# Attention followed by two mixture layers: another spread of the query rows over the partitions, other steps for score pairs and loads, another order of the first loads

## The chip, the cores and the metric

The kernel runs on one NeuronCore of one Trainium2 chip. The metric is the time of one execution on the device in microseconds (us), lower is better. The profile is one execution on the same chip type, whose own time stands beside its span below.

## The reference

Two batches, 12 heads, 448 positions, head size 64. Scores are mixed over the heads before the softmax (`w_pre`) and the probabilities are mixed over the heads after it (`w_post`); then come two dense layers of width 2048, one with ELU, one with SiLU.

```
scores = scale * q @ k.T                          # (b, h, i, j)
scores = einsum('bhij,hg->bgij', scores, w_pre)   # mix heads
attn   = exp(scores - max_j); attn = attn / (sum_j + 1e-9)
attn   = einsum('bhij,hg->bgij', attn, w_post)    # mix heads again
x      = (attn @ v) as (b*s, h*d)                 # 896 x 768
x      = elu(x @ moe_w_in) @ moe_w_out
out    = silu(x @ moe2_w_in) @ moe2_w_out
```

## The kernel before, in words

The order of every engine's work is the order of the program text (`manual_schedule`), so each engine and each queue is first in, first out.

**Query tiles and score pairs.** The 896 query rows (batch 0, then batch 1) are cut into seven tiles T = 0 to 6 of 128 rows; tile 3 holds the last 64 rows of batch 0 in partitions 0 to 63 and the first 64 of batch 1 in 64 to 127. `qk_pair(T, p)` (L128) computes the scores of heads 2p and 2p+1 for all rows of a tile into two PSUM banks, and `qk_evac` (L140) copies them, one on ScalarE and one on VectorE, into the tile `s` with one query row per partition and 12 x 448 values in it.

**Blocks and moves.** The head mixing wants (query, head) on the partitions. Each batch is therefore cut into 45 blocks of ten query rows (the last has eight), numbered through both batches, 90 in all. `move` (L153) copies one block by a DMA on SyncE's queue from `s` (ten partitions, 12 heads each) to `blk` (120 partitions, 448 values each). Where the rows of a block lie is fixed by `spread` (L40): the whole blocks of a tile lie interleaved, row i of the k-th block at partition i*n + k, where n is the number of whole blocks (12 in a full tile, 5 and 6 in the halves of tile 3), so the ten rows of one block are 12 (5, 6) partitions apart. The rows of blocks that are cut by a tile's edge, and the last eight rows of a batch, lie side by side behind them, and each such piece is a move of its own.

**Steps.** Step s of 45 handles blocks 2s and 2s+1: `premix` (L174, two PSUM banks, waits for the two moves of its blocks), row maximum (`rmax`, VectorE), exponentials (`exps`, ScalarE), `recip`, scaling of the post weights on GpSimd, and in the next step `postmix` (L212) and `post_evac`. `relayout(s + 2)` (L157) is called in step s, so moves run two steps ahead; `blk` has three buffers (`NBUF`), so a move waits until `premix` of three steps earlier has read its buffer. Step s also runs what dictionaries put there: `QK_AT` a score pair of a later tile, `X_AT` two attention-times-value pairs (`av_pair`, from step 8, mostly in even steps), `D_AT` loads on SyncE's queue: query tiles (`load_q`), the keys of batch 1 (`load_k(1, p)`), quarters of the values (`load_v`).

**Before the first step.** A tile of zeros is set, ScalarE writes one element of it (which loads its table), three matmuls of zeros run on TensorE (L290), keys of batch 0 and the first three query tiles are loaded on the SyncE and ScalarE queues, all six pairs of tile 0 are computed, the moves of steps 0 and 1 are issued, then three pairs of tile 1 (`LEAD`).

**After step 44** the two dense layers run, 36 to 96 matmuls in a row on TensorE, with weights that are loaded by SyncE.

```
for s in range(AHEAD): relayout(s)          # L296
...
premix(s); X_AT; QK_AT; postmix(s - 1); rmax(s); exps(s)
... qk_evac, recip, post_evac(s - 1); relayout(s + AHEAD); D_AT; M_AT   # L330
```

Of the kernel before, what the change touches and what calls it, by code (L numbers as in the profile page):

```python
# [7 lines left out]
F32 = mybir.dt.float32  # L8
# [4 lines left out]
AF = mybir.ActivationFunctionType  # L13
# [4 lines left out]
P = 128  # L18
B, H, S, D = 2, 12, 448, 64
# [3 lines left out]
NP = H // 2  # L23
CP = S // 4
BI = 10
# [3 lines left out]
HS = 64  # L29
BW = 5 * H  # L30
NBUF = 3
NWARM = 3
NE = 3
LEAD = 3
KO = (0, 2, 4, 1, 3, 5)
# [1 line left out]
KB = -(-S // BI)  # L37


def spread():  # L40

    tiles, blocks = [], {}
    for segs in ([(0, 0, 128)], [(0, 128, 256)], [(0, 256, 384)], [(0, 384, 448), (1, 0, 64)], [(1, 64, 192)], [(1, 192, 320)], [(1, 320, 448)]):
        T, base, of = len(tiles), 0, [None] * P
        for b, q0, q1 in segs:
            k0, k1 = -(-q0 // BI), q1 // BI
            n = k1 - k0
            for k in range(k0, k1):
                blocks[b, k] = [(T, base + k - k0, n, BI, 0)]
                for i in range(BI):  # L50
                    of[base + i * n + k - k0] = (b, k * BI + i)
            r = base + BI * n
            for x0, x1 in ((q0, k0 * BI), (k1 * BI, q1)):
                if x1 > x0:
                    blocks.setdefault((b, x0 // BI), []).append((T, r, 1, x1 - x0, x0 % BI))
                    for x in range(x0, x1):
                        of[r] = (b, x)
                        r += 1
            base += q1 - q0
        tiles.append((of, [b for b, _, _ in segs]))  # L60
    return tiles, blocks


QTILES, BLOCKS = spread()


@with_exitstack
def attn_moe_moe(ctx: ExitStack, tc: tile.TileContext, q, k, v, w_pre, w_post, w1i, w1o, w2i, w2o, out):
    nc = tc.nc
# [3 lines left out]
    def pool(name, **kw):  # L73
        cm = tc.tile_pool(name=name, reuse_waits="tile", **kw)
        return cm, cm.__enter__()

    cm_c, cp = pool("const", bufs=1, side="left")
# [3 lines left out]
    cm_w, wp = pool("qt", bufs=1, side="right")  # L81
# [5 lines left out]
    cm_ps, ps = pool("psA", bufs=1, space=PSUM)  # L87

    kpre = cp.tile([P, HS], F32, name="kpre")
    kps = cp.tile([P, H, 5], F32, name="kps")  # L90
    cp.tile([P, 24], F32, name="align2")
    vall = [ap_.tile([P, H, 4, D], F32, name=f"v{b}") for b in range(B)]
    blkb = ap_.tile([P, NBUF, 2, S], F32, name="blk")

    tiles = [(b, t) for b in range(B) for t in range(4)]
# [5 lines left out]
    qT, kT = {}, {}  # L101

    def load_q(T, eng=None, parts=(slice(0, NP),)):
        qT[T] = wp.tile([P, NP, 2 * P], F32, name=f"qt{T}", tag="qT", bufs=3).rearrange("p a b -> p (a b)")[:, :NP * P].rearrange("p (a b) -> p a b", a=NP)
        for p in parts:
            (eng or nc.sync).dma_start(qT[T][:, p], q[T, :, p])

    def load_k(b, p, eng=None):
        if b == 0:
            kT[p] = kp.tile([P, 2, S], F32, name=f"kt{p}", tag=f"kT{p}")  # L110
        (eng or nc.sync).dma_start(kT[p][:, b], k[b, p])

    def load_v(b, u, g):

        h = slice(3 * g, 3 * g + 3)
        o = slice(0, P) if u is None else slice(HS * u, HS * u + HS)
        nc.sync.dma_start(vall[b][o, h].rearrange("p h r d -> p (h r d)"), v[b, o, 768 * g:768 * g + 768])
# [10 lines left out]
    def qk_pair(T, p, where=("qk0", "qk1")):  # L128

        bs = QTILES[T][1]  # L130
        if T not in smap:
            smap[T] = (sp1, sp0)[T % 2].tile([P, H, S], F32, name=f"s{T}", tag="s")
        pq = [ps.tile([P, S], F32, name=f"pq{T}_{p}_{e}", tag=w, bufs=1) for e, w in enumerate(where)]
        for c in range(2):
            for e in range(2):
                half = slice(e * D, (e + 1) * D)
                nc.tensor.matmul(pq[e][HS * c:HS * c + HS], qT[T][half, p, HS * c:HS * c + HS], kT[p][half, bs[c % len(bs)]], start=True, stop=True, tile_position=(e * D, HS * c))  # L137
        sev.append((T, p, pq))

    def qk_evac(e):  # L140
        for T, p, pq in sev:
            o = smap[T][:, 2 * p + e]
            if e == 0:
                nc.scalar.activation(o, pq[0], AF.Copy, scale=0.125)  # L144
            else:
                nc.vector.tensor_scalar(o, pq[1], 0.125, None, op0=ALU.mult)
        if e == 1:
            sev.clear()

    seq = [(b, n) for b in range(B) for n in range(KB)]  # L150
    NB = len(seq) // 2

    def move(s, c, piece):  # L153
        T, r, d, m, i = piece
        nc.sync.dma_start(blkb[4 + H * i:4 + H * (i + m), s % NBUF, c], smap[T][r:r + d * (m - 1) + 1:d])

    def relayout(s):  # L157

        if s >= NB:
            return  # L160
        for c in range(2):
            x = BLOCKS[seq[2 * s + c]]
            for piece in x[len(x) - 1 if c == 0 else 0:]:
                move(s, c, piece)
        if s + 1 < NB:
            for piece in BLOCKS[seq[2 * s + 2]][:-1]:
                move(s + 1, 0, piece)

    def prow(s):
# [2 lines left out]
    pre, nmx, pexp, sums, kr, pst = {}, {}, {}, {}, {}, {}  # L172
# [9 lines left out]
    def rmax(s):  # L182
        n = prow(s)
        nmx[s] = ap_.tile([P, 2], F32, name=f"nmx{s}", tag="nmx", bufs=3)
        for r in range(2):
            nc.vector.tensor_reduce(nmx[s][:n, r:r + 1], pre[s][r][:n], axis=AX.X, op=ALU.max, negate=True)  # L186
# [83 lines left out]

    wz = sp0.tile([P, S], F32, name="wz", tag="s")
    nc.vector.memset(wz, 0.0)
    nc.scalar.activation(wz[0:1, 0:1], wz[0:1, 0:1], AF.Copy)
    load_k(0, 0, nc.scalar)
    load_q(0, parts=(slice(0, 2), slice(2, NP)))
    for p in range(1, NP):
        load_k(0, p, (nc.scalar, nc.sync)[p % 2])
    nc.scalar.dma_start(kpre, w_pre)
    nc.scalar.dma_start(kps.rearrange("p h i -> p (h i)"), w_post)
    load_q(1)  # L280
    load_q(2)
    for g in range(2):
        load_v(0, None, g)
    nc.gpsimd.memset(blkb[0:4], 0.0)
    for c in range(2):
        for r in range(2):
            nc.vector.memset(pbank[c][HS * (1 - r):HS * (2 - r), (4 * r + 3) * BW:(4 * r + 4) * BW], 0.0)
    for n in range(NWARM):
        pw = ps.tile([P, 4 * CP], F32, name=f"warm{n}", tag=f"pre{n % 3}", bufs=1)
        nc.tensor.matmul(pw, wz[:, :P], wz, start=True, stop=True)  # L290
    BANKS = (("qk0", "qk1"), ("pre0", "pre1"), ("pre2", "av"))
    for p in range(NP):
        qk_pair(0, p, BANKS[p % 3])
# [2 lines left out]
    for s in range(AHEAD):  # L296
        relayout(s)
# [6 lines left out]
    QK_AT, X_AT, D_AT = {}, {}, {}  # L304

    def at(d, step, f):
        d.setdefault(int(step), []).append(f)

    for T, n0 in enumerate((1 - LEAD, 4, 11, 17, 24, 30), 1):
        for p in range(LEAD if T == 1 else 0, NP):  # L310
            at(QK_AT, n0 + p, lambda T=T, p=p: qk_pair(T, p))
    for T in range(3, NQ):
        at(D_AT, (3, 9, 13, 19)[T - 3], lambda T=T: load_q(T))
    for T in range(NT_ - 1):
        for p in range(NP):
            nav = 8 + 6 * T + p // 2 * 2 if T < 5 else (38, 39, 40, 42, 43, 44)[3 * T + p // 2 - 15]
            at(X_AT, nav, lambda T=T, p=p: av_pair(T, p))
    for p in range(NP):
        at(D_AT, 6 + p, lambda p=p: load_k(1, p))
    for g in range(4):  # L320
        for u in range(2):
            for b in range(B):
                if b == 1 or g > 1:
                    at(D_AT, 2 * g + u + (16 if b else 0), lambda b=b, u=u, g=g: load_v(b, u, g))

    def run(d, s):
        for f in d.get(s, []):
            f()

    def step(s):  # L330
        if s < NB:
            premix(s)
        run(X_AT, s)
        run(QK_AT, s)
        run(F_AT, s)
        if 0 <= s - 1 < NB:
            postmix(s - 1)
        if s < NB:
            rmax(s)
            exps(s)  # L340
        two = s in X_AT
        if two:
            run(B_AT, s)
            if s < NB:
                recip(s)
            av_evac()
            av_split()
        qk_evac(0)
        qk_evac(1)
        if not two:  # L350
            run(B_AT, s)
            if s < NB:
                recip(s)
        if 0 <= s - 1 < NB:
            post_evac(s - 1)
        relayout(s + AHEAD)
        run(D_AT, s)
        run(M_AT, s)
# [230 lines left out]
    for i in range(2 * NE):  # L589
        n, j = divmod(i, 2)  # L590
# [40 lines left out]
    x1 = mo["x1"]  # L631
# [23 lines left out]
    h = {}  # L655
# [262 lines left out]
    n = NE  # L918
# [56 lines left out]
    x = [t[:, i] for t in rr for i in range(3)] + [xq[1, 5]] + [xq[1, p] for p in range(5)]  # L975
    xt[1] = {}
    for t, n_ in zip(x, "B11_0 B11_1 B11_2 T1_0 T1_1 T1_2 B21_0 B21_1 B22_0 T2_0 T2_1 B22_1 T3_0 T3_1 T4_0 T4_1 B21_2 T2_2 T3_2 T4_2 B22_2".split()):
        a, i = n_.split("_")
        xt[1][a, int(i)] = t
    for n in range(O1 + 8, I2):  # L980
        po = out_iter(n)
        if n == O1 + 9:
            y = mo["eg"][:1, 3, :1]
            nc.scalar.activation(y, y, AF.Silu)
        if po:
            c = chunks[n][2]
# [11 lines left out]
    x = [t[:, i] for t in rt for i in range(3)] + rk[:3]  # L998
# [3 lines left out]
    x = [ge[u][:, i] for u in range(2) for i in range(3)] + [gs[:, i] for i in range(6)]  # L1002
# [87 lines left out]
```

## Time and profile before

| | |
|---|---|
| median of 3 runs | 627.4 us (626.49 to 627.94) |
| the profiled execution | 626.38 us, span 624.6 us |
| TensorE matmul busy | 604.4 us (97%) |
| VectorE busy | 423.4 us (68%) |
| ScalarE busy | 363.2 us (58%) |
| GpSimd busy | 63.1 us (10%) |
| chain that ended last | PE 86%, DMA 7%, ACT 4%, DVE 2%, issue 1% |
| DMA | 82.03 MB, mean 131 GB/s |

Busy time is the union of an engine's instructions. The chain that ended last is followed back from the last instruction; its share of an engine is the time in which the program's end hung on that engine. The 45 steps take from 15 us to about 178 us of the span.

### The profile page before, as it was taken

What the parts mean: (1) busy time and instruction counts of PE and PEld (TensorE: products, weight loads), DVE (VectorE), ACT (ScalarE), POOL (GpSimd) and SP (SyncE); (2) the same over time, 40 slices, a digit from 0 to 9 for tenths busy, and PEclk for the clock granted to TensorE, in tenths of its full rate; (3) what the DMA queues carried; (4) which work ended last, traced back from release to release, by engine and by line L of the source; (5) the groups of instructions that cost most, each with busy time, mean ns of one, the idle gap of its engine ahead of it and who ended that gap; (6) DMA issues with size and microseconds to landing.
All of it is one profiled execution on the core that took longest, in us unless ns stands there. A gap on an engine that the chain in (4) does not pass through costs nothing.

```text
span 624.6 us, 14978 instructions
## 1 busy us (share of the span) xinstructions
PE 604.4 (97%) x6168; PEld 513.9 (82%) x6168; DVE 423.4 (68%) x717; ACT 363.2 (58%) x675; POOL 63.1 (10%) x117
## 2 busy tenths in 40 slices
PE   7899998998999999999999999999999999999997
PEld 3455654666689989999999999999999999999997
DVE  4766765787747799896776675599888877434420
ACT  4666765677856876657883554277676665332210
POOL 1222222226570000000000000000000000000000
PEclk9999999999999999999999999999999999999999
DMA  7586465555432235323244233434433423545300
GB/s 250 187 210 207 136 162 157 201 147 182 137 104 72 82 106 180 120 93 119 86 127 136 82 117 102 152 102 152 119 134 102 135 92 124 162 138 164 114 30 29
DMA packets 37588, 82.03 MB, mean 131 GB/s; under 512 B 4112, under 2 KB 18192, under 8 KB 37520
## 3 DMA queue, kind: packets, MB, share of 16 engines
q1 hardware_dynamic: 36656, 80.21, 41.3%
q8 instruction: 48, 0.79, 0.5%
q10 hardware_dynamic: 864, 0.87, 0.4%
q14 instruction: 20, 0.16, 0.1%
HBM read 59.05 MB, written 2.75 MB: 99 GB/s over the span
## 4 chain that ended last, share of the span: by engine, by line
PE 86%; DMA 7%; ACT 4%; DVE 2%; issue 1%; ACTq 0%; POOL 0%; DVEq 0%; SPq 0%; POOLq 0%
PE po L521 37%; PE b L795 27%; DMA blk<-s 7%; PE av L247 5%; PE pre L180 4%; PE post L219 4%; PE pq L137 3%; PE ph L507 3%; ACT pe L194 2%; PE post L507 1%; DVE nmx L186 1%; PE warm L290 1%; DVE a L123 1%; ACT gs L658 0%; ACT we L727 0%
## 5 line engine op out<-in xcount | busy, mean ns | idle before, releaser
L795 PE MATMUL b<-x,we 128*128 128x448 f32 x360 | 93.7, 363 | 0.0
L194 ACT ACTIVATE pe<-pre,nmx 124x448 f32<-124x448 f32 x90 | 56.3, 630 | 48.1 <-DVE nmx L186 47.2
L521 PE MATMUL po<-x,we 128*128 128x448 f32 x288 | 81.0, 362 | 0.0
L747 ACT ACTIVATE wr<-wr 128x768 f32<-128x768 f32 (+1 forms) x61 | 52.6, 864 | 41.9 <-DMA wr<-in_w2o_dram 26.9
L795 PEld LDWEIGHTS b<-x,we 128*128 128x128 f32 x360 | 67.5, 188 | 4.6 <-DVE we L527 0.2
L795 PE MATMUL b<-rr,we 128*128 128x448 f32 x288 | 69.5, 362 | 0.0
L478 DVE TENSOR_TENSOR we<-wc,we 128x640 fp32r<-128x640 f32 (+1 forms) x37 | 32.4, 875 | 48.3 <-ACT we L469 48.2
L219 PEld LDWEIGHTS post<-krn,pe 60*64 60x64 f32 x2520 | 46.9, 135 | 20.9 <-issue 10.5
L180 PE MATMUL pre<-blk,kpre 64*64 64x448 f32 (+1 forms) x360 | 54.4, 546 | 9.5 <-DMA blk<-s 6.9
L521 PE MATMUL po<-ge,we 128*128 128x448 f32 x216 | 60.3, 362 | 0.0
L186 DVE TENSOR_REDUCE nmx<-pre 124x1 f32<-124x448 f32 x90 | 51.5, 614 | 9.8 <-PE pre L180 9.4
L743 DVE SCALAR_TENSOR_TENSOR wc<-wr,wc 128x768 int32<-128x768 int32 (+1 forms) x62 | 56.2, 907 | 2.8
L521 PEld LDWEIGHTS po<-x,we 128*128 128x128 f32 x288 | 54.1, 188 | 3.5
L795 PEld LDWEIGHTS b<-rr,we 128*128 128x128 f32 x288 | 54.1, 188 | 3.5
L521 PE MATMUL po<-rr,we 128*128 128x448 f32 x216 | 55.9, 362 | 0.0
L521 PE MATMUL po<-gs,we 128*128 128x448 f32 x216 | 54.9, 362 | 0.0
L219 PE MATMUL post<-krn,pe 60*64 60x60 f32 x2520 | 48.6, 219 | 2.9 <-POOL krn L207 1.8
L207 POOL TENSOR_SCALAR krn<-kps,sum 124x60 f32<-124x60 f32 x90 | 37.8, 435 | 124.6 <-DVE sum L203 94.4
L247 PEld LDWEIGHTS av<-a,v 128*64 128x64 f32 x768 | 36.9, 137 | 15.9 <-ACT pe L194 7.0
L521 PE MATMUL po<-ta,we 128*128 128x448 f32 x168 | 44.8, 362 | 0.0
L469 ACT CAST we<-wc 128x640 fp32r<-128x640 f32 (+1 forms) x37 | 28.2, 764 | 27.9 <-DVE wc L743 26.7
L137 PE MATMUL pq<-kt,qt 64*64 64x448 f32 x336 | 43.0, 550 | 1.4 <-ACT s L144 1.4
(129 smaller groups left out, 1018.5 us busy)
## 6 DMA issues: line engine op xcount, KB each, us to landing
blk<-s SPq DMA_DIRECT2D x83, 210.0 KB
wr<-in_w1i_dram SPq DMA_DIRECT2D x32, 384.0 KB
wr<-in_w2i_dram SPq DMA_DIRECT2D x32, 384.0 KB
wr<-in_w1o_dram SPq DMA_DIRECT2D x24, 384.0 KB
wr<-in_w2o_dram SPq DMA_DIRECT2D x24, 384.0 KB
wr<-in_w1o_dram SPq DMA_DIRECT2D x12, 256.0 KB
wr<-in_w2o_dram SPq DMA_DIRECT2D x12, 256.0 KB
out_dram<-rk SPq DMA_DIRECT2D x11, 224.0 KB
```

What stands on the lines that cost most here:

```text
L137: nc.tensor.matmul(pq[e][HS * c:HS * c + HS], qT[T][half, p, HS * c:HS * c + HS], kT[p][half, bs[c % len(bs)]], start=True, stop=True, til ...
L180: nc.tensor.matmul(pre[s][r][HS * c:HS * c + HS], kpre[o], blkb[o, s % NBUF, c], start=True, stop=True, tile_position=(HS * r, HS * c))
L186: nc.vector.tensor_reduce(nmx[s][:n, r:r + 1], pre[s][r][:n], axis=AX.X, op=ALU.max, negate=True)
L194: nc.scalar.activation(t[:n], pre[s][r][:n], AF.Exp, bias=nmx[s][:n, r:r + 1], scale=1.0, accum_out=sums[s][:n, r:r + 1])
L207: nc.gpsimd.tensor_scalar(t[:n], kps[:n], z[:n, r:r + 1], None, op0=ALU.mult)
L219: nc.tensor.matmul(w[c][HS * u:HS * u + HS, r, j * BW:(j + 1) * BW], pexp[s][r][o, m * HS:(m + 1) * HS], kr[s][r][o].rearrange("p h i -> p ...
L247: nc.tensor.matmul(avt[T][e * D:(e + 1) * D, p % 2, :m], vall[b][:NV, h, j], amap[T][:NV, j * H + h, :m], start=j == 0, stop=j == 3, tile_ ...
L478: nc.vector.tensor_tensor(lo[:, :m], wbits[n][:, :m].bitcast(F32), hi[:, :m], op=ALU.subtract)
L521: nc.tensor.matmul(po, wt[:, kk * P:(kk + 1) * P], g_op(moe, k0 + kk, hf, gi), start=(k0 == 0 and n_ == 0), stop=(k0 + kn == KF and n_ == ...
L743: nc.vector.scalar_tensor_tensor(cc, r[:, :, 1], 3, cc, op0=ALU.logical_shift_left, op1=ALU.bitwise_or)
L747: nc.scalar.activation(hf, hf, AF.Prelu, scale=2.0 ** -112, alpha=2.0 ** 32)
L795: nc.tensor.matmul(o, wt[:, u * KH + i * P:u * KH + (i + 1) * P], X[x, i][:, xi], start=start and n_ == 0, stop=n_ == 8, skip_group_check= ...
```

## The change

Four things, all in the attention part.

1. **Rows.** `spread` now reads a table `CUTS`. In the six full tiles, the ten rows of a whole block lie 13 partitions apart (`(r, 13, BI)` for r = 0 to 10); the twelfth block has nine rows 13 apart and one row alone, which is a move of its own. Left-over rows lie 13 partitions apart as well. In tile 3 the rows of a block are 2, 3 or 4 apart, and the left-over pieces of batch 0 lie 2 apart. The last eight rows of batch 0 become two moves (seven rows and one).
2. **Steps.** The last three pairs of tile 1 run in steps 1, 1 and 2 (before: 1, 2, 3); those of tile 2 in steps 3 to 8 (before: 4 to 9). A second pair of a step waits for `qk_evac` of the first. Query tiles 3 to 6 are loaded in steps 8, 14, 18 and 24 (before: 3, 9, 13, 19), the keys of batch 1 in steps 8 to 13 (before: 6 to 11). The second quarter of batch 0's values is loaded in halves in steps 2 and 3 (before: ahead of the first step).
3. **First loads.** The first keys go on SyncE's queue and the first queries on ScalarE's, each as the first of its queue; the post weights move to SyncE's queue, between tile 1's and the values' load.
4. **Warm-up.** Two matmuls of zeros, of 448 and 224 columns, in place of three of 448. ScalarE's table load acts on another tile (`pad`), behind its loads, so that the zeros no longer pass through ScalarE.

`relayout` sends the early piece of a cut block ahead by a rule of its own (`early`), since a block can now have two pieces in one tile.

```diff
-NWARM = 3
+WHOLE = [[(r, 13, BI)] for r in range(11)] + [[(12, 13, 9), (115, 1, 1)]]
+FIRST = [[(14, 3, BI)], [(15, 3, BI)], [(16, 3, BI)], [(44, 2, BI)], [(45, 2, BI)]]
+SECOND = [[(64 + r, d, BI)] for r, d in ((1, 2), (2, 4), (4, 4), (23, 4), (25, 4), (44, 2))]
+CUTS = (
+    [(0, 0, 12, WHOLE, [], [(11, 13, 8)])],
+    [(0, 128, 12, WHOLE, [(11, 13, 2)], [(37, 13, 6)])],
+    [(0, 256, 12, WHOLE, [(11, 13, 4)], [(63, 13, 4)])],
+    [(0, 384, 5, FIRST, [(2, 2, 6)], [(1, 2, 7), (0, 1, 1)]), (1, 0, 6, SECOND, [], [(64, 21, 4)])],
+    [(1, 64, 12, WHOLE, [(11, 13, 6)], [(89, 13, 2)])],
+    [(1, 192, 12, WHOLE, [(11, 13, 8)], [])],
+    [(1, 320, 12, WHOLE, [], [(11, 13, 8)])],
+)
...
+    def early(n):
+        x = BLOCKS[seq[n]]
+        return [y for y in x if n % 2 == 0 and y[0] < x[-1][0]]
...
-    nc.scalar.activation(wz[0:1, 0:1], wz[0:1, 0:1], AF.Copy)
-    load_k(0, 0, nc.scalar)
-    load_q(0, parts=(slice(0, 2), slice(2, NP)))
-    for p in range(1, NP):
-        load_k(0, p, (nc.scalar, nc.sync)[p % 2])
+    nc.vector.memset(pad[0:1], 0.0)
+    for p in range(NP):
+        load_k(0, p, (nc.sync, nc.scalar)[p in (2, 4)])
+        if p < 2:
+            load_q(0, nc.scalar, (slice(0, 2), slice(2, NP))[p:p + 1])
     nc.scalar.dma_start(kpre, w_pre)
-    nc.scalar.dma_start(kps.rearrange("p h i -> p (h i)"), w_post)
+    nc.scalar.activation(pad[0:1], pad[0:1], AF.Copy)
     load_q(1)
+    nc.sync.dma_start(kps.rearrange("p h i -> p (h i)"), w_post)
+    load_v(0, None, 0)
     load_q(2)
-    for g in range(2):
-        load_v(0, None, g)
...
-    for n in range(NWARM):
-        pw = ps.tile([P, 4 * CP], F32, name=f"warm{n}", tag=f"pre{n % 3}", bufs=1)
-        nc.tensor.matmul(pw, wz[:, :P], wz, start=True, stop=True)
+    for n in range(2):
+        pw = ps.tile([P, 4 * CP], F32, name=f"warm{n}", tag=f"pre{n}", bufs=1)[:, :S >> n]
+        nc.tensor.matmul(pw, wz[:, :P], wz[:, :S >> n], start=True, stop=True)
...
-    for T, n0 in enumerate((1 - LEAD, 4, 11, 17, 24, 30), 1):
+    for T, n0 in enumerate((0, 3, 11, 17, 24, 30), 1):
         for p in range(LEAD if T == 1 else 0, NP):
-            at(QK_AT, n0 + p, lambda T=T, p=p: qk_pair(T, p))
+            at(QK_AT, (p - 1) // 2 if T == 1 else n0 + p, lambda T=T, p=p: qk_pair(T, p))
     for T in range(3, NQ):
-        at(D_AT, (3, 9, 13, 19)[T - 3], lambda T=T: load_q(T))
+        at(D_AT, (8, 14, 18, 24)[T - 3], lambda T=T: load_q(T))
...
-        at(D_AT, 6 + p, lambda p=p: load_k(1, p))
+        at(D_AT, 8 + p, lambda p=p: load_k(1, p))
...
-                if b == 1 or g > 1:
+                if b == 1 or g > 0:
...
-        run(QK_AT, s)
+        for i, f in enumerate(QK_AT.get(s, [])):
+            if i:
+                qk_evac(0)
+                qk_evac(1)
+            f()
```

## Rows read from the trace of the kernel before

**Rows 1.** The page, its part 4: the chain that ended last, by engine.

```profile
PE 86%; DMA 7%; ACT 4%; DVE 2%; issue 1%; ACTq 0%; POOL 0%; DVEq 0%; SPq 0%; POOLq 0%
```

**Rows 2.** That chain in order of time: start us, us, what.

```profile
12.06 2.83 DMA blk<-s
...
33.75 7.97 DMA blk<-s
...
48.44 8.56 DMA blk<-s
...
75.82 6.47 DMA blk<-s
...
89.25 6.66 DMA blk<-s
...
100.94 8.77 DMA blk<-s
```

**Rows 3.** Timeline of the start, all engines: start us, us, instructions, idle before.

```profile
0.89 0.43 DVE L272 MEMSET wz<- 128x448 f32 x1 [0.89 <-PEq L1076]
...
2.27 4.32 PE L290 MATMUL warm<-wz 128*128 128x448 f32 x6 [2.27 <-ACT wz L273]
...
15.02 2.67 PE L180 MATMUL pre<-blk,kpre 64*64 64x448 f32 x12 [1.18 <-DMA blk<-s]
...
23.27 0.55 PE L180 MATMUL pre<-blk,kpre 64*64 64x448 f32 x2
...
29.14 0.94 PE L180 MATMUL pre<-blk,kpre 64*64 64x448 f32 x8
```

**Rows 4.** TensorE's timeline, 36 to 62 us.

```profile
40.31 0.97 PE L180 MATMUL pre<-blk,kpre 64*64 64x448 f32 x4 [0.71 <-DMA blk<-s]
```

**Rows 5.** TensorE's timeline, 60 to 125 us.

```profile
62.03 0.94 PE L180 MATMUL pre<-blk,kpre 64*64 64x448 f32 x8
62.79 0.93 PE L137 MATMUL pq<-kt,qt 64*64 64x448 f32 x8
63.54 0.99 PE L219 MATMUL post<-krn,pe 60*64 60x60 f32 x56
64.36 0.94 PE L180 MATMUL pre<-blk,kpre 64*64 64x448 f32 x8
...
68.63 0.94 PE L180 MATMUL pre<-blk,kpre 64*64 64x448 f32 x8
...
75.23 0.94 PE L180 MATMUL pre<-blk,kpre 64*64 64x448 f32 x8
...
107.92 0.97 PE L180 MATMUL pre<-blk,kpre 64*64 64x448 f32 x4 [1.20 <-ACT xr L258]
...
116.18 0.98 PE L180 MATMUL pre<-blk,kpre 64*64 64x448 f32 x8
```

**Rows 6.** Line 155's moves on SyncE: count, issue ns min/median/max, first and last start.

```profile
L155 SPq DMA_DIRECT2D blk<-s x95: 672/777/2952, 12.1 to 166.8; - x95
```

**Rows 7.** DMA issues of the span: moves of a whole block.

```profile
blk<-s SPq DMA_DIRECT2D x83, 210.0 KB
```

**Rows 8.** DMA queues, 13.3 to 17.8 us: packets, MB, share of 16 engines.

```profile
q1 hardware_dynamic: 610, 1.02, 60.1%
```

**Rows 9.** DMA queues, 168.7 to 172.0 us.

```profile
q1 hardware_dynamic: 85, 0.14, 39.0%
```

**Rows 10.** SyncE's own timeline: issues, start us, us.

```profile
77.52 2.70 SPq L117 DMA_DIRECT2D v<-in_v_dram  x1
...
101.88 4.32 SPq L117 DMA_DIRECT2D v<-in_v_dram  x1
```

**Rows 11.** Stretches, line 137's busy PE and PEld alone, then clock, DMA share, GB/s.

```profile
2.20:4.00 1.80, 0.00 (x0) 0.00 (x0) 1.00 0.89 252
4.00:5.90 1.90, 0.00 (x0) 0.00 (x0) 1.00 1.04 395
5.90:6.60 0.70, 0.08 (x4) 0.08 (x8) 1.00 1.03 391
```

More of the change, by code (lines that the diff above doesn't have):

```diff
@@ L37 @@
 KB = -(-S // BI)
+WHOLE = [[(r, 13, BI)] for r in range(11)] + [[(12, 13, 9), (115, 1, 1)]]
[10 more added lines that the diff above has]
+)
 def spread():
     tiles, blocks = [], {}
[L43 to L60, printed above, removed]
+    for T, segs in enumerate(CUTS):
+        of = [None] * P
+        for b, q, n, whole, left, right in segs:
+            k = -(-q // BI)
+            for j, aps in [(k - 1, left)] + [(k + x, a) for x, a in enumerate(whole)] + [(k + n, right)]:
+                i = q % BI if aps is left else 0
+                for r, d, m in aps:
+                    blocks.setdefault((b, j), []).append((T, r, d, m, i))
+                    for x in range(m):
+                        of[r + d * x] = (b, j * BI + i + x)
+                    i += m
+        tiles.append((of, [x[0] for x in segs]))
     return tiles, blocks
@@ L90, in attn_moe_moe @@
     kps = cp.tile([P, H, 5], F32, name="kps")
-    cp.tile([P, 24], F32, name="align2")
+    pad = cp.tile([P, 24], F32, name="align2")
     vall = [ap_.tile([P, H, 4, D], F32, name=f"v{b}") for b in range(B)]
@@ L103, in load_q @@
     def load_q(T, eng=None, parts=(slice(0, NP),)):
-        qT[T] = wp.tile([P, NP, 2 * P], F32, name=f"qt{T}", tag="qT", bufs=3).rearrange("p a b -> p (a b)")[:, :NP * P].rearrange("p (a b) -> p a b", a=NP)
+        if T not in qT:
+            qT[T] = wp.tile([P, NP, 2 * P], F32, name=f"qt{T}", tag="qT", bufs=3).rearrange("p a b -> p (a b)")[:, :NP * P].rearrange("p (a b) -> p a b", a=NP)
         for p in parts:
@@ L161, in relayout @@
         for c in range(2):
-            x = BLOCKS[seq[2 * s + c]]
-            for piece in x[len(x) - 1 if c == 0 else 0:]:
-                move(s, c, piece)
+            gone = early(2 * s + c)
+            for piece in BLOCKS[seq[2 * s + c]]:
+                if piece not in gone:
+                    move(s, c, piece)
         if s + 1 < NB:
-            for piece in BLOCKS[seq[2 * s + 2]][:-1]:
+            for piece in early(2 * s + 2):
                 move(s + 1, 0, piece)
```

## Prediction

> **What bounds the kernel now.** I read the chain that ended last first: TensorE carries 86% of it, but 7% is DMA [rows 1]. In order of time that DMA share is a handful of pieces, all of them moves into `blk`, all before 110 us: 2.83 us ahead of step 0, then 7.97, 8.56, 6.47, 6.66 and 8.77 [rows 2]. The reader is to see the contrast: a move that starts with an idle queue lands after 2.83 us, the five others take two to three times as long. Behind 110 us the chain has no move, so the dense layers and the last third of the attention can only slide forward or back as a whole.
>
> TensorE's timeline then says what a step costs when no move is late. Steps 13 to 17 run as two pairs of steps of 6.60 us each [rows 5], with one attention-times-value group and two score pairs in each; a score pair is 0.75 us of it (62.79 to 63.54) and an odd step 2.33 [rows 5]. Before step 8, where there is no value work, a step takes 2.94 us (23.27 to 29.14, two steps), set by the chain from row maximum to exponentials to the post weights [rows 3].
>
> Against these prices: steps 8 to 12 run from 40.31 to 62.03, 21.7 us [rows 4, 5]. They hold three value groups and three score pairs: two pairs of steps at 6.60 less one score pair (5.85 each) and step 12 at 6.60 - 2.33 = 4.3, together 16.0. So 5.7 us are lost there. Steps 17 to 26 run from 75.23 to 116.18, 40.95 us [rows 5]; three pairs at 6.60, one with a single score pair (5.85) and the last with shorter value work (estimated at 6.2) make 31.85, so 9.1 us are lost. Only 1.20 of that is put down to something else than a move, ScalarE's copy at L258 [rows 5].
>
> **Why the moves are late.** There are 95 moves, 83 of whole blocks [rows 6, 7]; the other twelve are left-over pieces, whose rows now lie side by side. Two stretches of the DMA view show what that costs. From 13.3 to 17.8 us only moves of whole blocks are in flight: 610 packets take 60.1% of 16 engines over 4.5 us, 0.601 x 16 x 4.5 / 610 = 71 ns a packet [rows 8]. From 168.7 to 172.0 us only the last left-over piece (eight rows side by side) is: 85 packets at 39.0%, 0.39 x 16 x 3.3 / 85 = 242 ns [rows 9], 3.4 times as much with nothing else in flight. A row is twelve packets (12 heads); if one DMA engine carries a row, it spends 2.9 us on it and not 0.85, and what is queued behind it waits 2.05 us more. SyncE feels it too: the loads behind the left-over pieces take 2.70 and 4.32 us to issue [rows 10], against 0.78 for a median move [rows 6], and the next moves are queued behind them.
>
> The Trainium skill ("SBUF — State Buffer", Door 1: The DMA port swizzle) says that four neighbouring partitions share one of 16 DMA ports; by that rule eight neighbouring rows sit on two ports and would take four times as long as eight rows on eight ports. The two rows above give 3.4. The same rule speaks against a part of this change: partitions 0 to 63 reach only eight of the ports, so ten rows in one half of tile 3 meet in pairs whether they lie 5 and 6 apart or 2, 3 and 4 apart.
>
> **The change, part by part.**
>
> *Start.* The zeros are ready at 0.89 + 0.43 = 1.32, the warm-up starts only at 2.27 because it waits for ScalarE's write into them [rows 3]; that wait goes. The warm-up halves from 4.32 to 2.16, so it would run from about 1.4 to 3.6. The score pairs then need the first keys and a third of the first queries, 352 KB: 252 GB/s from 2.2 us gives 454 KB by 4.0 [rows 11], so they land at about 3.7 (an estimate). All of tile 0's inputs are 1.73 MB; at 395 and 391 GB/s [rows 11] they are there at about 7.4. Six pairs at 0.75 from 3.7, the first two at twice that, since the warm-up matmuls too take 0.72 us for 448 columns where a pair does eight such passes, four at a time, in 0.75: done at about 9.7, plus the last copy of 0.6: the first move at 10.3 and not 12.06 [rows 2]. The values' first quarter and tile 2's queries are still landing then, 0.1 us. Term: **-1.7** (bounds -2.4, +3.6 if the slow pace lasts through all nine pairs ahead of step 0).
>
> *Steps 0 to 7.* They took 40.31 - 15.02 = 25.3 us [rows 3, 4]. Steps 0 to 2 took 8.25 (15.02 to 23.27); five more at 2.94 make 22.95. A second pair in step 1 puts one copy more ahead of its maximum and its exponentials, at most 0.7. Then 23.65: **-1.6** (bounds 0, -2.3). What makes room: the values' halves stand alone in steps 2 to 7, keys and tile 3's queries no longer meet them, and the left-over pieces of tiles 0 and 1 read at 71 ns. The values' second quarter is added in steps 2 and 3, two halves of 192 KB with no other load beside them, in place of 384 KB ahead of step 0.
>
> *Steps 8 to 12.* At most the 5.7 lost. Queries and keys of tile 3 now land here, one key load a step beside two moves. Two moves hold an engine for 2 x 12 x 71 ns = 1.7 us of a 3.3 us step, a key load moves 224 KB, at 370 to 395 GB/s 0.6 us: 2.3 of 3.3, so it fits, except step 8 with queries as well (3.3). I take **-4.7** (bounds -1, -5.7). Tile 2's pairs end one step earlier, so their copies no longer hold the moves of step 12 back; step 9 holds no score pair for that, and step 3 one more, both priced at 0.
>
> *Steps 17 to 26.* Five left-over pieces (four to eight rows) lose 2.05 us each on the engines that carry them, 10 us in all, and the stalls of SyncE behind them. The queries of tile 5 come into this stretch (step 13 to 18), those of tile 6 stay in it (19 to 24); the value loads of batch 1 stay, one a step. Tile 3's whole blocks keep paired rows. Of 9.1 lost, 1.2 is ScalarE's; of the 7.9 left I take **-5.5** (bounds -2, -7.9).
>
> *Cost.* Seven moves more, six for a single row of a twelfth block and one at batch 0's end. On SyncE 7 x 0.78 = 5.4 us over 45 steps [rows 6]; two moves and a load are about 2.1 us of a 3.3 us step, so it lies in SyncE's idle time. Single rows are twelve packets. Taken at 0; without that cover 0.78 each where a move is awaited.
>
> Sum: -1.7 - 1.6 - 4.7 - 5.5 = -13.5 on the profiled execution's 626.4, which lies 1.0 under the median shown: 612.9, on the median's footing **613.9**. All bounds at their best give -18.3, 609 on the median's footing; at their worst +0.6.
>
> **The rivals.**
>
> *Only the first stretch is relieved.* Tile 3's blocks stay slow with one value load a step, and steps 17 to 26 keep their waits but for 1 us: -9.0, 618.4. For it: the chain has three of its late moves there [rows 2]. Against: the longest issue stalls stand behind left-over pieces [rows 10]. The skill's port rule above would have it so.
>
> *Loads come late.* Keys and queries of tile 3 are loaded three steps (9 us) before use and not five to eight. With a latency like the 8.56 us of a move at 48 us [rows 2] they are just in time; 2.5 us more, met twice (at step 11 by keys and queries, and again behind step 8's pile of loads), give -13.5 + 5 and 618.9.
>
> *Slow clock through the start.* TensorE idles between warm-up and first pairs, and its slow pace (0.72 us for 448 columns [rows 3], though the granted clock is recorded as 1.00, the 2.4 GHz level [rows 11]) lasts through tile 0 and three pairs: 7 x 0.75 = 5.3 later, 619.2. The Trainium skill ("TensorE: Matmul & The Clock Gate", What's actually happening) has the throttled clock as the state of an idle engine, released by activity; by that, less warm-up work makes this likelier.
>
> *No change.* Late moves were set by the number of DMAs in flight; what left-overs give back, seven more take: 627.
>
> *Slower.* The left-overs are slow because few rows go through few engines, not because they lie side by side. Then nothing is gained on twelve, and seven more small pieces cost 2.05 us each where step 5, 12, 18 and so on wait for their twelfth block: +14 less the 8 of start and steps 0 to 12: 633. It decides if a packet of a left-over piece still takes over 150 ns. Against: fewer engines at work would lower the sum that is moved, but not lengthen a packet to 242 ns [rows 9].
>
> **How the numbers follow.** Forecast 0.60; first stretch only 0.15; late loads 0.07; slow clock 0.06; no change 0.04; slower 0.08. Below 0.2% (1.3 us), about what a measurement of this kernel can tell from no change, I call it the same. Faster is 0.60 + 0.15 + 0.07 + 0.06 = 0.88, same 0.04, slower 0.08. The likeliest case's own range is 609 to 617; the three at 618 to 619 must be in, with the bounds of their terms: 605 to 621, leaving out the last two cases and a little at the lower end, where step pairs that I priced from rows fall shorter still.
>
> **What would show it.** The first move near 10.3 us; step 8's premix near 37.0, step 13's near 54.0, step 27's near 102.7; no move of over 5 us in the chain behind step 0; packets near 75 ns when a left-over piece is alone; no issue of over 2 us on SyncE before 110 us; the dense layers as long as before. The prediction is wrong if the new waits sit on the twelfth block's second piece, or if steps without late moves turn out longer than 2.9 us because copies of score pairs stand ahead of the maximum.

## The result, and the profile after

The changed kernel takes **618.87 us** (median of six runs, 617.61 to 621.21) against 627.66 us for the kernel before on the same chip; the ratio is 0.987 with a 95% interval of 0.9844 to 0.9897. That is 8.2 us less by the ratio, which is used below (8.8 by the two medians): inside the range of 605 to 621, five above the forecast of 613.9, and nearest to the rival in which only the first stretch is relieved (618.4).

The profiled execution took 621.21 us with a span of 619.4. It was the slowest of the six, so a second execution of the same kernel (618.0 us of span) is read beside it below. In two of the twelve runs told below (start alone, and the queries loaded earlier) the profiled execution was about 2% longer than the fast ones of the same kernel, so of these two runs only the times of the fast executions are used.

The page's part 4, the chain that ended last by engine, answers to [rows 1]:

```profile
PE 86%; ACT 5%; DMA 4%; DVE 3%; issue 1%; SPq 0%; ACTq 0%; DVEq 0%
```

The chain in order of time answers to [rows 2]. DMA fell from 7% to 4%. Of five late moves the first two (7.97 and 8.56 us) are gone altogether; those behind 75 us are not: 10.37 us in two moves and 4.08 stand where 6.47, 6.66 and 8.77 stood (5.65, 5.69 and 4.70 in the second execution).

```profile
10.61 2.83 DMA blk<-s
...
23.72 2.46 DMA blk<-s
...
26.27 1.80 issue
...
80.30 10.37 DMA blk<-s x2
...
99.41 4.08 DMA blk<-s
```

TensorE's timeline answers to [rows 3 to 5]. The premixes (line 193, line 180 before) of steps 0, 4, 5, 8, 13, 17 and 27 are shown; the bracket is idle time ahead of the instruction and what ended it.

```profile
13.58 3.09 PE L193 MATMUL pre<-blk,kpre 64*64 64x448 f32 x14 [1.26 <-DMA blk<-s]
...
25.42 0.94 PE L193 MATMUL pre<-blk,kpre 64*64 64x448 f32 x8
28.90 1.37 PE L145 MATMUL pq<-kt,qt 64*64 64x448 f32 x8 [2.54 <-ACT s L152]
...
31.50 1.73 PE L193 MATMUL pre<-blk,kpre 64*64 64x448 f32 x8
...
40.82 0.54 PE L193 MATMUL pre<-blk,kpre 64*64 64x448 f32 x1
...
58.35 0.94 PE L193 MATMUL pre<-blk,kpre 64*64 64x448 f32 x8
...
71.54 0.94 PE L193 MATMUL pre<-blk,kpre 64*64 64x448 f32 x8
...
112.07 0.59 PE L193 MATMUL pre<-blk,kpre 64*64 64x448 f32 x3
```

The same lines of the second execution of the changed kernel:

```profile
14.72 3.12 PE L193 MATMUL pre<-blk,kpre 64*64 64x448 f32 x14 [1.27 <-DMA blk<-s]
...
26.61 0.94 PE L193 MATMUL pre<-blk,kpre 64*64 64x448 f32 x8
...
30.43 0.98 PE L193 MATMUL pre<-blk,kpre 64*64 64x448 f32 x8
...
39.90 0.54 PE L193 MATMUL pre<-blk,kpre 64*64 64x448 f32 x1
...
57.84 0.94 PE L193 MATMUL pre<-blk,kpre 64*64 64x448 f32 x8
...
71.32 0.94 PE L193 MATMUL pre<-blk,kpre 64*64 64x448 f32 x8
...
110.59 0.98 PE L193 MATMUL pre<-blk,kpre 64*64 64x448 f32 x8
```

Subtracting starts gives the stages in us. The other columns are experiments told below, read in the same way.

| | before | after | after, again | rows alone | steps alone | rows and start | forecast |
|---|---|---|---|---|---|---|---|
| step 0 starts | 15.0 | 13.6 | 14.7 | 14.9 | 15.4 | 14.2 | 13.3 |
| steps 0 to 7 | 25.3 | 27.2 | 25.2 | 23.3 | 28.9 | 23.3 | 23.7 |
| steps 8 to 12 | 21.7 | 17.5 | 17.9 | 23.6 | 18.1 | 20.5 | 17.0 |
| steps 13 to 16 | 13.2 | 13.2 | 13.5 | 13.2 | 13.4 | 13.2 | 13.2 |
| steps 17 to 26 | 40.95 | 40.5 | 39.3 | 38.6 | 40.5 | 38.0 | 35.5 |

Steps 8 to 12 took the time that was forecast. Steps 0 to 7 gained nothing, and steps 17 to 26 gained 0.4 to 1.7 us and not 5.5. The dense layers are as long as before, within 0.8 us.

DMA queues from 164.2 to 165.9 us, where but for the end of the moves before it only the last left-over piece is in flight (eight rows, now 13 apart), answer to [rows 9]:

```profile
q1 hardware_dynamic: 116, 0.18, 29.3%
```

0.293 x 16 x 1.7 / 116 = 69 ns a packet against 242. The trace's single packets of 1792 bytes say the same: half of them took 74 ns or less here, and 273 ns or less in the window of [rows 9]. So the left-over pieces were slow because their rows lay side by side: it is the same number of rows.

The moves on SyncE (count, issue ns min/median/max, first and last start) answer to [rows 6], all of the span and then those from 80 to 90 us; SyncE's own timeline (start us, us) answers to [rows 10]:

```profile
L163 SPq DMA_DIRECT2D blk<-s x102: 662/782/2215, 10.6 to 163.2; - x102
...
L163 SPq DMA_DIRECT2D blk<-s x7: 779/817/2215, 79.4 to 89.5; - x7
```

```profile
82.52 5.02 SPq L163 DMA_DIRECT2D blk<-s  x3
```

The issues of 2.70 and 4.32 us behind left-over pieces are gone; the longest of all moves is 2.215. But it lies between 80 and 90 us, where three moves take 5.02 together: this stretch still holds SyncE up, though left-over rows no longer lie side by side.

### The profile page after: what moved, and what is told of

The parts are those of the page before. It is cut to its first block, busy times and chain, and to the rows that moved or that the text cites. A ratio compares the mean times of both kernels' runs of the same rounds, so it can differ in the third digit from the quotient of the medians.

```text
span 619.4 us, 14985 instructions
## 1 busy us (share of the span) xinstructions
PE 600.7 (97%) x6166; PEld 514.0 (83%) x6166; DVE 422.6 (68%) x718; ACT 362.9 (59%) x675; POOL 63.1 (10%) x117
## 3 DMA queue, kind: packets, MB, share of 16 engines
q1 hardware_dynamic: 36749, 80.08, 40.5%
## 4 chain that ended last, share of the span: by engine, by line
PE 86%; ACT 5%; DMA 4%; DVE 3%; issue 1%; SPq 0%; ACTq 0%; DVEq 0%
PE po L538 37%; PE b L812 27%; PE av L260 4%; PE pre L193 4%; PE pq L145 4%; PE post L232 4%; DMA blk<-s 4%; PE ph L524 3%; ACT pe L207 3%; PE post L524 1%; DVE nmx L199 1%; DVE a L131 1%; DMA qt<-in_q_dram 1%; DVE sum L215 0%; ACT gs L675 0%
## 5 line engine op out<-in xcount | busy, mean ns | idle before, releaser
L193 PE MATMUL pre<-blk,kpre 64*64 64x448 f32 x360 | 50.6, 554 | 5.7 <-ACT xr L271 3.0
L260 PEld LDWEIGHTS av<-a,v 128*64 128x64 f32 x768 | 36.9, 137 | 15.8 <-ACT pe L207 7.8
```

Source lines behind the costliest of these rows:

```text
L193: nc.tensor.matmul(pre[s][r][HS * c:HS * c + HS], kpre[o], blkb[o, s % NBUF, c], start=True, stop=True, tile_position=(HS * r, HS * c))
L260: nc.tensor.matmul(avt[T][e * D:(e + 1) * D, p % 2, :m], vall[b][:NV, h, j], amap[T][:NV, j * H + h, :m], start=j == 0, stop=j == 3, tile_ ...
```

## The experiments

All are variants of one of the two kernels and compute all of it. A gain is (1 - ratio) x 627.5.

### Which part brings the time

**Rows alone.** The kernel before with the table of rows and `early`, nothing else.

```diff
+WHOLE = [[(r, 13, BI)] for r in range(11)] + [[(12, 13, 9), (115, 1, 1)]]
...
+    def early(n):
```

> The kernel before with the new table of rows alone (103 or so moves, no other edit). Theory A (rows side by side were slow to read, and what stood behind them waited): the left-over pieces land about 2.5 us sooner, the first stretch of late moves (steps 7 to 13) shrinks, 3 to 6 us faster than before. Rival (small pieces are slow as such, seven more of them cost): no gain or up to 5 us slower.

Measured: ratio 0.9895 (0.9854 to 0.9936), 6.6 us gained, a little more than expected.

**Steps alone.** The kernel before with the new steps of pairs and loads.

```diff
-    for T, n0 in enumerate((1 - LEAD, 4, 11, 17, 24, 30), 1):
+    for T, n0 in enumerate((0, 3, 11, 17, 24, 30), 1):
...
-        at(D_AT, (3, 9, 13, 19)[T - 3], lambda T=T: load_q(T))
+        at(D_AT, (8, 14, 18, 24)[T - 3], lambda T=T: load_q(T))
```

> The kernel before with the new steps alone: score pairs of tiles 1 and 2 earlier, queries, keys and a quarter of the values in other steps. Theory A: fewer loads meet the moves in steps 3 to 11, but the copies of tile 2's first pair, now in step 3, must wait until the last left-over piece of tile 0 (eight rows side by side, slow) has left the same buffer, some 3 to 5 us; the two about cancel, between 3 us faster and 2 us slower. Rival (spreading the loads is what the change lives on): 5 to 8 us faster.

Measured: 0.9985 (0.9964 to 1.0006), 0.9 us, not told from nothing. Its stages differ all the same. Steps 8 to 12 fall from 21.7 to 18.1 us, with the left-over rows still side by side; TensorE's timeline, steps 8 and 13:

```profile
44.27 0.54 PE L180 MATMUL pre<-blk,kpre 64*64 64x448 f32 x1
...
62.39 0.94 PE L180 MATMUL pre<-blk,kpre 64*64 64x448 f32 x8
```

Its chain has no move of over 3 us between 36 and 76 us, so the late move of 8.56 us is gone; the next one is this:

```profile
76.33 6.43 DMA blk<-s
```

Steps 0 to 7 give it back: steps 4 to 5 alone take 7.50 us (27.32 to 34.82), by the wait that is told further down.

**Start alone.** The kernel before with the new order of first loads and the shorter warm-up.

```diff
-    nc.scalar.activation(wz[0:1, 0:1], wz[0:1, 0:1], AF.Copy)
+    nc.vector.memset(pad[0:1], 0.0)
...
-    for n in range(NWARM):
+    for n in range(2):
```

> The kernel before with the new order of the first loads and the shorter warm-up alone. Theory A: the first move starts 1.4 us sooner, and as steps 0 to 7 follow a chain, all of it is kept: 1.2 to 1.6 us faster. Rival (the late moves of steps 7 to 13 take it back, as they hang on the loads and not on the start): 0 to 0.5 us.

Measured: 0.9975 (0.9943 to 1.0007), 1.6 us, not told from nothing either, though it is the size of the forecast's term.

**Rows and start, without the steps.** The changed kernel with the pairs and loads in the steps of before.

```diff
-    for T, n0 in enumerate((0, 3, 11, 17, 24, 30), 1):
+    for T, n0 in enumerate((1 - LEAD, 4, 11, 17, 24, 30), 1):
...
-        at(D_AT, 8 + p, lambda p=p: load_k(1, p))
+        at(D_AT, 6 + p, lambda p=p: load_k(1, p))
```

> The changed kernel with the steps of before: the new rows and the new start without the new steps. Theory A, as it stands after the runs so far (rows about 6.5, start about 1.5, steps about 1, of which tile 2's early copies and step 1's second pair take back some): 7 to 9 us faster than before, within 1.5 us of the changed kernel. Rival (the parts need each other, rows without the new steps leave the moves late): under 6.5 us faster.

Measured: 0.9881 (0.9857 to 0.9905), 7.5 us, as much as the whole change. Its TensorE timeline, steps 8, 13, 17 and 27:

```profile
37.54 0.54 PE L193 MATMUL pre<-blk,kpre 64*64 64x448 f32 x1
...
58.07 0.94 PE L193 MATMUL pre<-blk,kpre 64*64 64x448 f32 x8
...
71.26 0.94 PE L193 MATMUL pre<-blk,kpre 64*64 64x448 f32 x8
...
109.31 0.98 PE L193 MATMUL pre<-blk,kpre 64*64 64x448 f32 x8
```

Its chain still has a late move in this stretch, ahead of step 10, though no left-over rows lie side by side:

```profile
39.16 7.13 DMA blk<-s
```

So the new steps are worth nothing on top of the rows in the whole time. By the table they give 2.6 to 3.0 us in steps 8 to 12 and take back 1.9 in steps 0 to 7 (25.2 against 23.3) and 1.3 in steps 17 to 26 (39.3 against 38.0).

### What steps 0 to 7 lost

Between the premixes of steps 4 and 5 lie 6.08 us in the profile after, where rows and start alone have 2.94. The all-engine timeline there shows the first copies of tile 2's scores, on ScalarE and VectorE, late behind idle time whose end this view does not name:

```profile
28.30 0.54 ACT L152 ACTIVATE s<-pq 128x448 f32<-128x448 f32 x1 [2.04 <-issue]
28.38 0.62 DVE L154 TENSOR_SCALAR s<-pq 128x448 f32<-128x448 f32 x1 [3.04 <-issue]
```

Tile 2's `s` takes the buffer of tile 0 (L140, one buffer for the even tiles). With its first pair in step 3, that pair's copies stand ahead of `relayout(5)`, which still moves blocks 10 and 11 and a piece of block 12 out of tile 0; they have to wait for the last of these moves, the piece of block 12, issued at 23.72. The chain credits this move with 2.46 us and calls the rest issue, but the semaphore updates in the trace are plainer: the one that the copies wait for takes its last arrival from this move at 28.00, and the first copy starts 0.30 us behind.

**Tile 2 one step later.**

```diff
-    for T, n0 in enumerate((0, 3, 11, 17, 24, 30), 1):
+    for T, n0 in enumerate((0, 4, 11, 17, 24, 30), 1):
```

> The changed kernel with tile 2's score pairs back in steps 4 to 9. Theory A (in step 3 their copies wait for the last piece of tile 0 to leave the buffer that tiles 0 and 2 share, which costs 2 to 3.5 us): 2 to 3.5 us faster than the changed kernel, about 616, and no copy of tile 2 with 2 us or more of idle time before it. Rival (that stall is a freak of the profiled execution, or comes back later): within 0.8 us of the changed kernel.

Measured: 0.9864 (0.9833 to 0.9895), the same as after. Its TensorE timeline has no such gap any more (26.21 to 29.24, steps 4 and 5):

```profile
26.21 0.54 PE L193 MATMUL pre<-blk,kpre 64*64 64x448 f32 x1
...
29.24 0.54 PE L193 MATMUL pre<-blk,kpre 64*64 64x448 f32 x1
```

**The changed kernel again**, without an edit, since the gap could be that one execution's.

> The changed kernel once more, unchanged, as the measure for the other three on the same chip. Theory A (tile 2's first copies wait in step 3 for tile 0's last piece): a gap of 5 to 6 us between the starts of steps 4 and 5 again, where a step takes 2.9. Rival (that gap is a freak of one execution): under 4 us. Either: 617 to 620 us.

Measured: 0.9893 (0.9859 to 0.9928), 6.7 us gained. The gap is 3.82 us (26.61 to 30.43, above): the wait costs about 0.9 us as a rule and cost 3 in the first profile. Three further variants with this pair in step 3, told below, have 3.83 to 3.86. The place was right, the price that was put on it was one execution's.

The same semaphore updates price the piece of block 12 itself, eight rows, from its issue to the last arrival: 5.7 us before and 5.6 with steps alone, rows side by side; 3.1 with rows alone, 3.0 with rows and start and 2.7 in this second execution, rows 13 apart; 4.3 in the first profile, where the three moves ahead of it took 3.8 to 4.8 us too (2.6 to 2.7 in the second execution).

### What steps 17 to 26 kept

**The values of batch 1 eight steps later**, in steps 24 to 31, behind the stretch.

```diff
-                    at(D_AT, 2 * g + u + (16 if b else 0), lambda b=b, u=u, g=g: load_v(b, u, g))
+                    at(D_AT, 2 * g + u + (24 if b else 0), lambda b=b, u=u, g=g: load_v(b, u, g))
```

> The changed kernel with the values of batch 1 loaded in steps 24 to 31, not 16 to 23. Theory B (in steps 19 to 25 the moves of tile 3's blocks and the value loads together fill the DMA engines): steps 17 to 26 shrink from 40.5 to 35 or 37 us, 3 to 5 us faster than the changed kernel. Rival C (tile 3's rows, two to a port in half of the partitions, are alone enough to hold the steps): under 1.5 us faster.

Measured: 0.9857 (0.9823 to 0.9891), 9.0 us; the interval overlaps that of the changed kernel in the same set. The stretch, steps 17 and 27 on TensorE's timeline, is 37.2 us, 2.1 less than in the second execution of after:

```profile
70.71 0.94 PE L193 MATMUL pre<-blk,kpre 64*64 64x448 f32 x8
...
107.88 0.98 PE L193 MATMUL pre<-blk,kpre 64*64 64x448 f32 x8
```

Steps 29 and 30 then take 9.45 us and not 7.66, so 1.8 of it comes back where the loads went. With the loads out of the way the DMA view from 86 to 92 us holds moves of tile 3 and nothing else:

```profile
DMA packets 516, 0.86 MB, mean 143 GB/s; under 512 B 37, under 2 KB 516, under 8 KB 516
...
q1 hardware_dynamic: 516, 0.86, 54.8%
...
blk<-s SPq DMA_DIRECT2D x5, 210.0 KB
```

0.548 x 16 x 6 / 516 = 102 ns a packet, between the 71 of full tiles [rows 8] and the 242 of adjacent rows [rows 9].

**Both, tile 2 and values late.**

```diff
-    for T, n0 in enumerate((0, 3, 11, 17, 24, 30), 1):
+    for T, n0 in enumerate((0, 4, 11, 17, 24, 30), 1):
...
-                    at(D_AT, 2 * g + u + (16 if b else 0), lambda b=b, u=u, g=g: load_v(b, u, g))
+                    at(D_AT, 2 * g + u + (24 if b else 0), lambda b=b, u=u, g=g: load_v(b, u, g))
```

> Both: tile 2's score pairs in steps 4 to 9 and batch 1's values in steps 24 to 31. If the two waits are apart, the gains add: theory A and B together 4 to 6 us faster than the changed kernel, about 613 to 615. If the rivals hold, under 1.5 us.

Measured: 0.985 (0.9817 to 0.9883), 9.4 us; the expected sum of the two was missed. Its stretch, 36.9 us, holds an idle time of TensorE in step 26 that no wait in the profile explains; at that place no other profile has one of over 1.3 us:

```profile
107.65 0.39 PE L232 MATMUL post<-krn,pe 60*64 60x60 f32 x10 [2.56 <-issue]
```

**Queries of tiles 5 and 6 loaded earlier again**, in steps 13 and 19.

```diff
-        at(D_AT, (8, 14, 18, 24)[T - 3], lambda T=T: load_q(T))
+        at(D_AT, (8, 14, 13, 19)[T - 3], lambda T=T: load_q(T))
```

> The changed kernel with the queries of tiles 5 and 6 loaded in steps 13 and 19 as before, not 18 and 24. Theory B (each load that the change brought into steps 17 to 26 costs what it occupies, about 1 us): 1 to 2 us faster than the changed kernel. Rival C: within 0.8 us.

Measured: 0.9884 (0.9846 to 0.9922), 7.3 us: nothing gained.

**Tile 3's whole blocks side by side.** The ten rows of each of the eleven blocks adjacent, all else as after.

```diff
-FIRST = [[(14, 3, BI)], [(15, 3, BI)], [(16, 3, BI)], [(44, 2, BI)], [(45, 2, BI)]]
+FIRST = [[(14 + BI * r, 1, BI)] for r in range(5)]
-SECOND = [[(64 + r, d, BI)] for r, d in ((1, 2), (2, 4), (4, 4), (23, 4), (25, 4), (44, 2))]
+SECOND = [[(64 + BI * r, 1, BI)] for r in range(6)]
...
-    [(0, 384, 5, FIRST, [(2, 2, 6)], [(1, 2, 7), (0, 1, 1)]), (1, 0, 6, SECOND, [], [(64, 21, 4)])],
+    [(0, 384, 5, FIRST, [(2, 2, 6)], [(1, 2, 7), (0, 1, 1)]), (1, 0, 6, SECOND, [], [(124, 1, 4)])],
```

> The changed kernel with the ten rows of each whole block of tile 3 side by side (and the four left-over rows of batch 1 too); the other six tiles as they are. Theory C2 (in steps 19 to 25 the time is set by how many rows of a block are read through the same port; two rows a port cost 102 ns a packet in a run without other loads, against 71): four rows a port cost about 240 ns, 2.9 us a block and 5.8 us or more a step in place of 3.5, so steps 17 to 26 grow by 12 to 18 us and the whole by as much. Rival (the moves' number or the value loads set it): under 3 us slower.

Measured: 1.0076 (1.0046 to 1.0106), slower than the kernel before and some 12 us slower than after. Steps 17 to 26 take 52.5 us by its TensorE timeline:

```profile
69.31 0.94 PE L193 MATMUL pre<-blk,kpre 64*64 64x448 f32 x8
...
121.80 0.98 PE L193 MATMUL pre<-blk,kpre 64*64 64x448 f32 x8
```

The chain in order of time holds four late moves there:

```profile
72.54 7.57 DMA blk<-s
...
81.00 6.06 DMA blk<-s
...
90.12 5.48 DMA blk<-s
...
100.34 7.16 DMA blk<-s
```

How the rows lie decides this stretch, then; it is not only the number of loads.

**Tile 3's whole blocks six apart**, with two left-over pieces of four adjacent rows as the price.

```diff
-FIRST = [[(14, 3, BI)], [(15, 3, BI)], [(16, 3, BI)], [(44, 2, BI)], [(45, 2, BI)]]
+FIRST = [[(r, 6, BI)] for r in range(5)]
-SECOND = [[(64 + r, d, BI)] for r, d in ((1, 2), (2, 4), (4, 4), (23, 4), (25, 4), (44, 2))]
+SECOND = [[(64 + r, 6, BI)] for r in range(6)]
...
-    [(0, 384, 5, FIRST, [(2, 2, 6)], [(1, 2, 7), (0, 1, 1)]), (1, 0, 6, SECOND, [], [(64, 21, 4)])],
+    [(0, 384, 5, FIRST, [(5, 6, 6)], [(41, 6, 4), (60, 1, 4)]), (1, 0, 6, SECOND, [], [(124, 1, 4)])],
```

> The changed kernel with the rows of tile 3's whole blocks six apart in both halves, as batch 1's were before, and its left-over rows six apart too but for two pieces of four rows side by side. Theory C2: of ten rows two pairs share a port now and four did, the two adjacent pieces cost 2 us each; about even, within 2 us of the changed kernel, and packets of whole blocks of tile 3 a little shorter. Rival: no difference in packets.

Measured: 0.9869 (0.9849 to 0.9889), the same as after; the packets of its blocks could not be read alone. Its stretch, steps 17 and 27 below, is 37.2 us, 2.1 and 3.4 less than in the two executions of after:

```profile
70.54 0.94 PE L193 MATMUL pre<-blk,kpre 64*64 64x448 f32 x8
...
107.71 0.98 PE L193 MATMUL pre<-blk,kpre 64*64 64x448 f32 x8
```

So six apart may be better than 2 to 4 apart for this stretch; one execution, its run's fastest, does not show it, and the whole time does not tell the two apart.

**Loads spread.** Tile 2 late, batch 1's values in steps 14 to 17 and 26 to 29, queries of tiles 4 and 6 in steps 13 and 26.

```diff
-    for T, n0 in enumerate((0, 3, 11, 17, 24, 30), 1):
+    for T, n0 in enumerate((0, 4, 11, 17, 24, 30), 1):
...
-        at(D_AT, (8, 14, 18, 24)[T - 3], lambda T=T: load_q(T))
+        at(D_AT, (8, 13, 18, 26)[T - 3], lambda T=T: load_q(T))
...
-                    at(D_AT, 2 * g + u + (16 if b else 0), lambda b=b, u=u, g=g: load_v(b, u, g))
+                    at(D_AT, 2 * g + u + ((14 if g < 2 else 22) if b else 0), lambda b=b, u=u, g=g: load_v(b, u, g))
```

> The changed kernel with tile 2's pairs in steps 4 to 9, batch 1's values in steps 14 to 17 and 26 to 29, and the queries of tiles 4 and 6 in steps 13 and 26: no load but one query tile in the steps of tile 3's blocks and none doubled behind them. Theory B: steps 17 to 26 at 36 to 37 us and no wait at steps 29 to 31 (as with values in 24 to 31): 3 to 5 us faster than the changed kernel, 614 to 616. Rival (what is saved there comes back elsewhere): 617 or more.

Measured: 617.8 us, 0.9853 (0.9836 to 0.987), 9.2 us. The stretch falls to 35.6 us, the forecast's number, and the whole gains one or two over after at most: steps 29 and 30 take 9.0 us.

```profile
71.49 0.94 PE L193 MATMUL pre<-blk,kpre 64*64 64x448 f32 x8
...
107.09 0.98 PE L193 MATMUL pre<-blk,kpre 64*64 64x448 f32 x8
...
113.78 0.57 PE L193 MATMUL pre<-blk,kpre 64*64 64x448 f32 x2
...
122.76 0.98 PE L193 MATMUL pre<-blk,kpre 64*64 64x448 f32 x8 [1.14 <-ACT xr L271]
```

## Why the prediction was right in sign and too high in gain

**The cause was right for most of the gain.** Left-over rows side by side cost 242 ns a packet; 13 apart they cost 69, and the table of rows alone gives 6.6 of the 8.2 us. It was not right for every late move that the prediction put down to it (steps 8 to 12 and 17 to 26 below). The slower rival, few rows through few engines, set its point at 150 ns and is out. The seven moves more cost nothing that shows, as forecast: full stages such as steps 13 to 16 kept their 13.2 us.

**Start, forecast -1.7.** The first move went out at 10.61 us (10.3 forecast) and step 0 came 1.4 us earlier in one execution, 0.3 in the other, where a key load ended a wait of 0.52 us on TensorE. Over nine profiled executions with the new start, the first move goes out at 10.4 to 11.75 us (median 11.3) and step 0 begins at 13.4 to 14.7 (median 14.25), against 14.9 to 15.4 in three with the old one (median 15.0): 0.8 us, half of the term. Start alone gave 1.6 with an interval that takes in nothing, which does not tell 0.8 from 1.7. The rival of the slow clock there did not come: the granted clock stayed at 1.00, and all nine pairs ahead of step 0 ran from 4.12 to 12.31 with the first move in between.

**Steps 0 to 7, forecast -1.6, measured 0 to +1.9.** Two pieces. The rows did bring 2.0 (23.3 in both variants without the new steps). The sentence that failed is the one that priced tile 2's earlier pairs "at 0": it followed the queries, the banks and TensorE, and not the buffer of `s`, which tile 0 still holds in step 3. That wait is 0.9 us as a rule; with the old rows (steps alone) it made steps 4 to 5 take 7.50 us. The second pair of step 1 was priced at up to 0.7 and took about that (4.8 us from step 1 to 2 against 4.1).

**Steps 8 to 12, forecast -4.7, measured -3.8 to -4.2.** Right in size, but not by the cause that "Why the moves are late" gave. Steps alone, with every left-over row still side by side, has 3.6 of it; rows alone has none (23.6 us, an unexplained idle time in it), and rows and start 1.2, with a move of 7.13 us still late there. So most of this term came from the new steps of pairs and loads and only some from the rows; that the size fitted is luck in part. With tile 2's pairs back in their old steps (tile 2 one step later) the stretch is still 18.1 us, so the moved loads are the likelier part; which of them was not tried. The late-loads rival is out: keys and queries of tile 3, loaded three steps ahead of use, end no wait of over 0.2 us.

**Steps 17 to 26, forecast -5.5, measured -0.4 to -1.7.** This is the mis-sized term, below the bound of -2 that was given. The working put the loss down to five left-over pieces, and left out what else is slow in this stretch; spreading their rows brought 2.4 to 2.9 us (rows alone, rows and start). Three things are now priced, from one execution each. First, tile 3's blocks, ten rows in one half of the partitions, take 102 ns a packet and move 143 GB/s; side by side they cost some 12 us more, and six apart the whole time is not told apart from after's. Second, the value loads of batch 1 cost some 2 us there. Third, the new steps themselves: 38.0 us without them, 39.3 with. The rival that was put at 0.15 described this, tile 3 still slow with one value load a step. Three of the signs named ahead failed here too: moves of over 5 us in the chain, an issue of over 2 us (2.215), and step 27's premix at 112.07 and 110.59 and not near 102.7. That the time lies in the stated range all the same owes much to the range, which was widened to hold the rivals at 618 to 619.

The Trainium skill ("SBUF — State Buffer", Door 1: The DMA port swizzle) lets partitions 0 to 63 reach only half of the ports, so that ten rows there would meet in pairs at some of them; the 102 ns against 71 agree in direction. So do the single packets in the trace of the values late (86 to 92 us): of 479 packets of 1792 bytes, 288 took under 80 ns and 103 took 140 to 160, twice the 74 of a spread piece, where from 13 to 17 us of the profile after 539 of 540 took under 100. That the half is the reason was argued so and not tried: no run had tile 3's blocks spread over all partitions. The prediction cited this rule as one that speaks against the change and still took 5.5 of 7.9 us. A chance of 0.15 for it was too little.

What stays open: the 2.5 us or so that steps 17 to 26 still lie over the priced floor in the best variant (35.6 against 31.85 and 1.2 of ScalarE), and why the moves behind the gap of steps 4 and 5 took 1 to 2 us longer in the first profile than in the second. That the new steps gain nothing over rows and start is shown by times to about 1.5 us, not closer. No variant beat the changed kernel by more than its intervals; the two best lie 1 to 2.5 us below it.

## What to carry to other kernels

When a transfer goes between SBUF partitions, price its packets by how the partitions are spread, and measure one piece alone in a window: here 69, 102 and 242 ns for the same bytes. When work is moved a step earlier, list the buffers that it writes and who still reads them, not only its inputs and engines. And a load that is moved out of a crowded stretch pays only if the stretch that receives it has room: here 1.8 of 2.1 us came back three steps later. Last, read every stage in the variants that hold one part of the change alone: in steps 8 to 12 the forecast time came from another part than the one it was priced on.

## What the runs showed of the hardware that was not expected

In the profile after, TensorE's clock fell once inside the attention. Two neighbouring stretches, from 25 and from 29 us (columns: PE, PEld, DVE, ACT, POOL busy, then granted clock, DMA share, GB/s):

```profile
25.00:29.00 4.00, 1.46 (x52) 0.69 (x42) 0.96 (x3) 1.97 (x6) 0.00 (x0) 1.00 0.65 201
29.00:33.00 4.00, 4.00 (x72) 2.32 (x76) 3.31 (x10) 2.69 (x7) 1.35 (x4) 0.58 0.65 169
```

After the 2.54 us of idle time ahead of 28.90 the mean granted clock was 0.58, near the 1.2 GHz level and not 2.4, and the premix of step 5 took 1.73 us and not 0.94. In the second execution, with 0.97 us idle at that place, the same premix took 0.98. A wait of 2.5 us can thus cost more than itself. The Trainium skill ("TensorE: Matmul & The Clock Gate", What's actually happening) describes the throttled clock as the state that idleness brings, which these two rows bear out. The length of one idle time does not settle it here: ahead of 107.65 in the variant with tile 2 and values late TensorE idled for 2.56 us and its granted clock stayed at 1.00, while with tile 3's rows side by side the clock fell behind one of 1.88 us (0.60 from 90 to 94 us).

The kernel with rows alone shows such a fall (0.60 from 53 to 55 us) behind an idle time that no wait of another engine explains:

```profile
53.32 0.48 PE L232 MATMUL post<-krn,pe 60*64 60x60 f32 x9 [2.40 <-issue]
```

What TensorE waited for in those 2.40 us, and in the 2.56 us of the other variant, is not settled. A 16 KB packet of an instruction queue began 0.4 and 0.2 us ahead of them (at 50.51 and 104.86); that it is the cause is not shown. With the slow clock behind it, it is much of why that variant's steps 8 to 12 are 23.6 us in the table, above the kernel before: steps 10 and 11 take 10.5 us, where rows and start have 7.2.
